# First stages of an attention-and-FFN kernel: transposing loads gated on the first weight chunk, q projections run six tiles behind k, and wq loaded right behind wk

## The chip, the core and the metric

The kernel runs on one core of a Trainium2 chip. The metric is the device time of one execution in microseconds (us). Time before: 278.08 us, the median of 3 runs (277.39 to 278.48).

## The reference, cut to what matters

```python
x = A_x                                            # [1, 2048, 640] bf16
g = sigmoid((x * gate_w).sum(-1, keepdims=True))
qkv = x @ wqkv                                     # wqkv [640, 1920]; 32 heads of 20
pq, pk = phi(q), phi(k)     # phi(t) = where(t > 0, t + 1, exp(t)) + 1e-6
kv = einsum("bhsd,bhse->bhde", pk, v);  z = einsum("bhsd->bhd", pk)
a = (pq @ kv / (pq . z + 1e-6)) @ wo
b = (gelu(x @ w_gate) * (x @ w_up)) @ w_down       # F = 1728
out = g * a + (1 - g) * b
```

The first stage, which the change touches, makes k and q of 16 tiles of 128 rows. For each tile it needs xT, the tile transposed, and the weights wk or wq, which are five chunks (of 128 rows) each.

## The kernel before

Tiles 0 to 2 are loaded plainly and transposed on TensorE (`T`). Tiles 3 to 15 are loaded by transposing DMAs on the SP queue. wk comes on the ACT queue. All k tiles come first, then all q tiles. Item `n` of the sequence uses two PSUM banks out of four pairs, so item n waits for the DVE pass `phi2` of item n-4.

```python
for k in range(KC):                                  # KC = 5
    dma_in(wk[:, k, :], A_wqkv[k*128:(k+1)*128, 640:1280], [r_wk[k]], eng="act")
for i in range(NXN):                                 # NXN = 3, on SP
    dma_in(x_aug[:, i, 0:640], A_x[0, i*128:(i+1)*128, :], [r_xn[i]])
for i in range(NXN, NT):                             # 13 transposing loads, on SP
    load_xT(i)
# ... the other loads, on SP ...
def KM(i, ks):   # k of tile i: per chunk one matmul of 512 and one of 128 columns
    ...          # reads r_xT[i] and r_wk[k]
def QM(i): ...   # q of tile i: reads r_xT[i], r_wq
def phi1(n): ... # ACT: Exp of the two banks
def phi2(n): ... # DVE: two instructions, frees the banks

warm(6, 512)     # six matmuls of 512 columns on a constant
T(0)
warm(2, 128)
T(1)
warm(2, 128)
KM(0, [0])
T(2)
# ... transpose of gate_w ...
KM(1, [0])
for k in range(1, KC):
    KM(0, [k]); KM(1, [k]); KM(2, [k - 1])
KM(2, [KC - 1])
for n in range(2 * NT):
    if n >= NT:  QM(n - NT)
    elif n >= 3: KM(n, list(range(KC)))
    phi1(n)
    phi2(n)
    if n == 3:   # wq, one load of 800 KB, on the ACT queue behind the fourth Exp
        dma_in(wq[:, :, 0:640], A_wqkv[:, 0:640].rearrange(...), [r_wq], eng="act")
```

## Time and profile before

| what | value | view |
|---|---|---|
| PE busy | 270.1 of 275.9 us (98%) | page, busy times |
| chain that ended last | 95% PE | page, chain |
| wk chunk 3: issue to landing | 2.75 to 8.99 us | chain in order of time |
| PE idle at that wait | 0.7 us | waits |
| first k of tile 3, 4, 5 starts | 10.95, 12.32, 13.69 us | timeline, counting pairs |
| k or q of a tile | 5 pairs of 0.27 us = 1.36 us | timeline |

The page: busy time by engine, and the shares of the chain that ended last.

```profile
PE 270.1 (98%) x1663; PEld 140.4 (51%) x1696; DVE 138.5 (50%) x233; ACT 78.3 (28%) x132; POOL 26.1 (9%) x28
...
PE 95%; DMA 2%; issue 1%; ACTq 1%; DVE 0%
```

The chain in order of time (start us, duration us, what): the part before 9 us. The load that it passes through is wk chunk 3.

```profile
2.75 6.24 DMA pool<-in_A_wqkv_dram
...
9.04 0.39 PE ps L419
```

The timeline of PE (start us, duration us, engine, line, operation; in brackets the idle time before and its releaser). L387 is a warm-up, L403 a `T`, L419 the 512-column and L420 the 128-column half of a k pair. In the first pair the halves start 0.42 us apart; from 6.25 us on they start 0.22 us apart, and a pair takes 0.27 us. That is the fastest spacing in these traces, called full rate below.

```profile
4.63 0.42 PE L387 MATMUL ps<-const-bfloat16-1.0 128*128 128x128 bf16 x2
4.85 0.63 PE L419 MATMUL ps<-pool 128*128 128x512 bf16 x1
5.27 0.31 PE L420 MATMUL ps<-pool 128*128 128x128 bf16 x1
5.49 0.71 PE L403 MATMUL ps<-pool 128*128 128x128 bf16 x5
...
6.25 0.39 PE L419 MATMUL ps<-pool 128*128 128x512 bf16 x1
6.47 0.22 PE L420 MATMUL ps<-pool 128*128 128x128 bf16 x1
...
9.04 0.39 PE L419 MATMUL ps<-pool 128*128 128x512 bf16 x1 [0.72 <-DMA pool<-in_A_wqkv_dram]
```

The loads of wk chunk 3 (issued 2.75) and of tile 3's transposing load (issued 2.20), one line each, from the view of DMA issues cut to 2.75 us; the last number is us from issue to landing.

```profile
pool<-in_A_wqkv_dram ACTq DMA_DIRECT2D x1, 160.0 KB, 6.2
pool<-in_A_x_dram SPq DMA_TRANSPOSE x1, 7.3
```

### The profile page before, as it was taken

What the parts mean: (1) busy time and instruction counts of PE and PEld (TensorE: products, weight loads), DVE (VectorE), ACT (ScalarE), POOL (GpSimd) and SP (SyncE); (2) the same over time, 40 slices, a digit from 0 to 9 for tenths busy, and PEclk for the clock granted to TensorE, in tenths of its full rate; (3) what the DMA queues carried; (4) which work ended last, traced back from release to release, by engine and by line L of the source; (5) the groups of instructions that cost most, each with busy time, mean ns of one, the idle gap of its engine ahead of it and who ended that gap; (6) DMA issues with size and microseconds to landing.
All of it is one profiled execution on the core that took longest, in us unless ns stands there. A gap on an engine that the chain in (4) does not pass through costs nothing.

```text
span 275.9 us, 4048 instructions
## 1 busy us (share of the span) xinstructions
PE 270.1 (98%) x1663; PEld 140.4 (51%) x1696; DVE 138.5 (50%) x233; ACT 78.3 (28%) x132; POOL 26.1 (9%) x28
## 2 busy tenths in 40 slices
PE   8899999999999999999999999999999999999996
PEld 5455555555545444444444444444555555555553
DVE  2398888510234324999999998535000122212223
ACT  1355555210431454223222223224555100000000
POOL 5000000000000401242432422000000000000000
PEclk9999999999999999999999999999999999999999
DMA  7998997002120111122121221380000010111111
GB/s 178 172 199 238 395 402 244 12 6 44 23 48 21 50 46 54 25 46 48 26 49 24 47 50 24 60 309 14 0 0 2 24 47 26 48 50 48 50 48 48
DMA packets 36400, 22.38 MB, mean 81 GB/s; under 512 B 25759, under 2 KB 34975, under 8 KB 36383
## 3 DMA queue, kind: packets, MB, share of 16 engines
q1 hardware_dynamic: 34997, 20.49, 27.4%
q10 hardware_dynamic: 1386, 1.64, 2.2%
q8 instruction: 13, 0.21, 0.3%
q14 instruction: 4, 0.03, 0.0%
HBM read 13.11 MB, written 2.62 MB: 57 GB/s over the span
## 4 chain that ended last, share of the span: by engine, by line
PE 95%; DMA 2%; issue 1%; ACTq 1%; DVE 0%
PE ps L596 41%; PE ps L739 20%; PE ps L702 6%; PE ps L432 6%; PE ps L503 6%; PE ps L419 5%; DMA pool<-in_A_wqkv_dram 2%; PE ps L505 2%; PE ps L433 2%; PE ps L703 2%; PE ps L420 2%; PE ps L571 2%; PE ps L723 1%; ACTq L331 1%; PE ps L617 1%
## 5 line engine op out<-in xcount | busy, mean ns | idle before, releaser
L596 PE MATMUL ps<-pool 128*128 128x512 bf16 x509 | 113.0, 379 | 0.6
L596 PEld LDWEIGHTS ps<-pool 128*128 128x128 bf16 x520 | 50.4, 98 | 60.0 <-issue 0.3
L739 PE MATMUL ps<-pool 128*128 128x128 bf16 (+1 forms) x407 | 56.6, 297 | 0.6 <-issue 0.2
L604 DVE TENSOR_TENSOR pool<-ps,pool 128x512 bf16<-128x512 f32 x52 | 35.8, 688 | 33.6 <-PE ps L596 30.4
L602 ACT ACTIVATE pool<-ps 128x512 f32<-128x512 f32 x52 | 31.1, 597 | 72.5 <-PE ps L596 72.1
L750 DVE SCALAR_TENSOR_TENSOR pool<-ps,pool 128x512 bf16<-128x512 f32 (+1 forms) x32 | 16.2, 547 | 63.8 <-PE ps L739 63.8
L739 PEld LDWEIGHTS ps<-pool 128*128 128x128 bf16 x416 | 31.8, 98 | 25.3 <-issue 1.1
L648 POOL TENSOR_TENSOR pool<-pool 128x640 f32<-128x640 bf16 x16 | 22.5, 1409 | 140.1 <-DMA pool<-z_row 87.1
L441 ACT ACTIVATE pool<-ps 128x640 bf16<-128x640 f32 x32 | 22.3, 704 | 23.1 <-PE ps L420 13.5
L454 DVE SCALAR_TENSOR_TENSOR pool<-ps,pool 128x640 bf16<-128x640 f32 x32 | 26.4, 825 | 2.2
L656 DVE TENSOR_TENSOR pool<-pool 128x640 bf16<-128x640 bf16 x16 | 23.0, 1441 | 0.6
L419 PE MATMUL ps<-pool 128*128 128x512 bf16 x77 | 21.9, 383 | 0.7 <-DMA pool<-in_A_wqkv_dram 0.7
L432 PE MATMUL ps<-pool 128*128 128x512 bf16 x77 | 21.4, 379 | 0.0
L702 PE MATMUL ps<-pool 128*128 128x512 bf16 x77 | 21.3, 379 | 0.0
L503 PE MATMUL ps<-pool 128*128 128x512 bf16 x76 | 21.2, 379 | 0.0
L505 PE MATMUL ps<-pool 128*128 128x129 bf16 x80 | 17.6, 220 | 0.2
L420 PE MATMUL ps<-pool 128*128 128x128 bf16 x80 | 17.6, 220 | 0.2
L433 PE MATMUL ps<-pool 128*128 128x129 bf16 x80 | 17.6, 220 | 0.2
L703 PE MATMUL ps<-pool 128*128 128x128 bf16 x80 | 17.5, 219 | 0.2
L707 ACT ACTIVATE pool<-ps,pool 128x640 f32<-128x640 f32 x16 | 12.7, 794 | 9.2 <-PE ps L703 9.2
L451 DVE TENSOR_SCALAR pool<-pool 128x640 bf16<-128x640 bf16 x32 | 10.4, 325 | 7.4 <-ACT pool L441 5.8
L419 PEld LDWEIGHTS ps<-pool 128*128 128x128 bf16 x80 | 7.9, 98 | 10.2 <-DMA pool<-in_A_wqkv_dram 1.0
(51 smaller groups left out, 130.7 us busy)
## 6 DMA issues: line engine op xcount, KB each, us to landing
out_dram<-pool SPq DMA_DIRECT2D x15, 160.0 KB, 1.8
pool<-in_B_w_gate_dram SPq DMA_DIRECT2D x1, 2080.0 KB, 13.6
pool<-in_B_w_up_dram SPq DMA_DIRECT2D x1, 2080.0 KB, 18.3
pool<-in_A_x_dram SPq DMA_DIRECT2D x1, 1280.0 KB, 8.3
pool<-in_B_w_down_dram SPq DMA_DIRECT2D x1, 1120.0 KB, 6.0
pool<-in_A_wo_dram SPq DMA_DIRECT2D x6, 160.0 KB, 8.8
pool<-in_B_w_down_dram SPq DMA_DIRECT2D x1, 960.0 KB, 8.5
pool<-in_A_wqkv_dram ACTq DMA_DIRECT2D x5, 160.0 KB, 4.4
```

Source lines behind the costliest of these rows:

```text
L419: e.matmul(ps[:, b0, :], lhs, wk[:, k, 0:512], start=(k == 0), stop=(k == KC - 1))
L420: last = e.matmul(ps[:, b1, 0:128], lhs, wk[:, k, 512:640], start=(k == 0), stop=(k == KC - 1))
L432: e.matmul(ps[:, b0, :], lhs, wq[:, k, 0:512], start=(k == 0), stop=(k == KC - 1))
L433: last = e.matmul(ps[:, b1, 0:129], lhs, wq[:, k, 512:641], start=(k == 0), stop=(k == KC - 1))
L454: P.op("dve", lambda e: e.scalar_tensor_tensor(dst, ps_flat[:, b0 * 512:b0 * 512 + 640], 1.0 + EPS, e_buf[m], ALU.add, ALU.max), reads=[ba ...
L503: e.matmul(ps[:, bs[n], :], lhs, x_aug[:, i, 0:512], start=(i == 0), stop=(i == NT - 1))
L505: last = e.matmul(ps[:, bt, n * 129:(n + 1) * 129], lhs, x_aug[:, i, 512:641], start=(i == 0 and n == 0), stop=(i == NT - 1), skip_group_c ...
L596: last = e.matmul(ps[:, b, :], w[:, k, fc * 128:(fc + 1) * 128], xT[:, k, j * 512:(j + 1) * 512], start=(k == 0), stop=(k == KC - 1))
L602: P.op("act", lambda e: e.activation(ge[n], ps[:, gb, :], ACT.Gelu_apprx_tanh), reads=[bank[gb]], writes=[r_ge[n]])
L604: P.op("dve", lambda e: e.tensor_tensor(hT[fc][:, j * 512:(j + 1) * 512], ps[:, ub, :], ge[n], ALU.mult), reads=[bank[ub], r_ge[n]], write ...
L702: e.matmul(ps[:, b0, :], lhs, w2[:, m, 0:512], start=(m == 0), stop=(m == KC - 1))
L739: last = e.matmul(dst, lhs, wd[:, fc, c0:c0 + cn], start=False, stop=(fc == NFC - 2), skip_group_check=True)
```

## The change

Its intent: let wk land before the transposing loads start; let q run only six tiles behind k, so that from tile 6 on a new xT is wanted for every second item alone and need not come so fast; and have wq early enough for that.

```diff
+KLEAD = 6
@@ loads
+dma_in(wq[:, :, 0:640], A_wqkv[:, 0:640]..., r_wq, reads=[r_wk[KC - 1]], eng="act")
 for i in range(NXN, NT):
-    load_xT(i)
+    load_xT(i, after=([r_wk[0]] if i == NXN else ()))
@@ order: k0..k5, then q0 k6 q1 k7 ... q9 k15, then q10..q15
+seq = [("k", i) for i in range(KLEAD)]
+for i in range(KLEAD, NT):
+    seq += [("q", i - KLEAD), ("k", i)]
+seq += [("q", i) for i in range(NT - KLEAD, NT)]
@@ head
-warm(6, 512)
+warm(5, 512)
 T(0)
-warm(2, 128)
+warm(3, 128)
 T(1)
-warm(2, 128)
 KM(0, [0])
+KM(1, [0])
 T(2)
 # ... transpose of gate_w ...
-KM(1, [0])
@@ loop
-    if n == 3:
-        dma_in(wq[:, :, 0:640], ..., [r_wq], eng="act")
```

(`phi1`, `phi2` and the bank slots now index `seq`; r_wq became five resources.)

More of the change, by code (lines that the diff above doesn't have):

```diff
@@ L301, in bass_gated_mix__linear_attn_block__geglu_ffn__prompt_kernel @@
             r_wk = [P.sb("wk%d" % k, R_WK + k * 640, R_WK + (k + 1) * 640) for k in range(KC)]
-            r_wq = P.sb("wq", R_WQ, R_WQ + KC * XW)
+            r_wq = [P.sb("wq%d" % k, R_WQ + k * XW, R_WQ + k * XW + 640) for k in range(KC)]
             r_gcol = P.sb("gcol", R_WQ, R_WQ + KC * XW)
@@ L339, in bass_gated_mix__linear_attn_block__geglu_ffn__prompt_kernel @@
                 dma_in(x_aug[:, i, 0:640], A_x[0, i * 128:(i + 1) * 128, :], [r_xn[i]])
+            dma_in(wq[:, :, 0:640], A_wqkv[:, 0:640].rearrange("(k p) w -> p k w", p=128), r_wq,
+                   reads=[r_wk[KC - 1]], eng="act")
             def load_xT(i, after=()):
@@ L410, in T, with KM @@
                     reads=[bank[tb]], writes=[r_xT[i]])
-            def KM(i, ks):
-                b0, b1 = slot(i)
+            seq = [("k", i) for i in range(KLEAD)]
+            for i in range(KLEAD, NT):
+                seq += [("q", i - KLEAD), ("k", i)]
+            seq += [("q", i) for i in range(NT - KLEAD, NT)]
+            def KM(n, ks):
+                i = seq[n][1]
+                b0, b1 = slot(n)
                 def fn(e):
@@ L423, in KM, with QM @@
                 P.op("pe", fn, reads=[r_xT[i]] + [r_wk[k] for k in ks], writes=[bank[b0], bank[b1]])
-            def QM(i):
-                b0, b1 = slot(NT + i)
+            def QM(n):
+                i = seq[n][1]
+                b0, b1 = slot(n)
                 def fn(e):
@@ L435, in fn @@
                     return last
-                P.op("pe", fn, reads=[r_xT[i], r_wq, r_gcol], writes=[bank[b0], bank[b1]])
+                P.op("pe", fn, reads=[r_xT[i], r_gcol] + r_wq, writes=[bank[b0], bank[b1]])
             def phi1(n):
@@ L442, in phi1 @@
                      reads=[bank[b0], bank[b1]], writes=[r_e[m]])
-                if n >= NT:
-                    i = n - NT
+                kind, i = seq[n]
+                if kind == "q":
                     P.op("act", lambda e: e.activation(eg[:, i:i + 1], ps[:, b1, 128:129], ACT.Tanh, scale=0.5),
@@ L452, in phi2 @@
                      reads=[r_e[m]], writes=[r_e[m]])
-                dst, r_dst = (pk[n], r_pk[n]) if n < NT else (pq[n - NT], r_pq[n - NT])
+                kind, i = seq[n]
+                dst, r_dst = (pk[i], r_pk[i]) if kind == "k" else (pq[i], r_pq[i])
                 P.op("dve", lambda e: e.scalar_tensor_tensor(
@@ L476, in bass_gated_mix__linear_attn_block__geglu_ffn__prompt_kernel @@
             for n in range(2 * NT):
-                if n >= NT:
-                    QM(n - NT)
+                if seq[n][0] == "q":
+                    QM(n)
                 elif n >= 3:
@@ L482, in bass_gated_mix__linear_attn_block__geglu_ffn__prompt_kernel @@
                 phi2(n)
-                if n == 3:
-                    dma_in(wq[:, :, 0:640], A_wqkv[:, 0:640].rearrange("(k p) w -> p k w", p=128), [r_wq],
-                           eng="act")
                 if n == 6:
```

## The prediction

> **What bounds the kernel.** TensorE: in the page's busy table PE has 270.1 of 275.9 us, and the chain that ended last is 95% PE. In the waits, PE waits after 12.4 us for nothing but 0.2 us of issue. Only the first 9 us, before the chain is unbroken matmuls, can shrink.
>
> **That start.** The chain runs through the ACT queue's wk loads into wk chunk 3, issued at 2.75 us, landing at 8.99 (6.24 us); its first matmul starts at 9.04, after 0.7 us of PE idle. By the issue-to-landing times the chunks land at about 4.4, 5.7, 6.6, 9.0, 9.4. The first transposing load is issued at 2.20 and lands 7.3 us later. From 2.5 to 5 us there are 85 DMA packets under 512 B and 312 GB/s; from 5 to 6 us, 387 and 207 GB/s, with the DMA share near 1. So transposing packets take the engines when the last wk chunks need them. The Trainium skill, "DMA: Bandwidth & Descriptors", section "Issuing engines are not separate DMA queues", says that loads of all issuers interleave on the same 16 engines; the trace agrees.
>
> **What the change does.**
> 1. Transposing loads start at wk 0's landing, about 4.4 instead of 2.2. Half of wk has moved by 5.0 (queue 10: 0.42 MB); the rest at 300 GB/s takes 1.3 us more: all wk by about 6.5 (estimate).
> 2. PE without waiting for wk: T(0) to T(2) and k of tiles 0 and 1 with chunk 0 until about 6.4; chunk 3's first matmul near 8.2 instead of 9.04. Gain 0.8 to 1.0 us, all critical.
> 3. Two warm-up matmuls fewer (0.43 and 0.21 us): they fill waiting time; about nothing.
> 4. q six tiles behind k: the same matmuls (1.36 us a tile), Exp (0.70), DVE (0.32 + 0.82). xT is wanted half as fast from tile 6 on, but PE did not wait for it before: 0.
> 5. wq is issued at about 6.5 instead of 12.5. Before, it took 7.1 us among transposing loads, so it lands near 14; the first q matmul wants it near 14.0. Stall 0 to 0.6 us, expected 0.2.
> 6. On ACT the wq issue waits for wk 4, ahead of the 1.28 us table load (before: at 3.72, hidden). First Exp not before wk 4 + 0.4 + 1.28, about 8.2; k of tile 0 ends near 9.1: hidden. But tile 4's k already waited for tile 0's DVE pass (0.17 us at 12.31), so beyond about 7.4 each us that wk 4 is later costs PE a us.
> 7. xT3, issued at 4.4 with 3.2 to 5 us to land, is there at 7.6 to 9.4; wanted near 10: small risk.
>
> **Sum.** -0.9 + 0.2 (wq) + 0.1 (xT3, table): about -0.7 us on 278.08, 277.35. Range 276.3 to 278.4 (runs of one kernel spread from 277.39 to 278.48). Within 2%: 0.98; faster 0.01; slower 0.01.
>
> **What would show it.** (1) The last two wk chunks landing in under 5 us; no PE wait for wqkv before 9 us. (2) Every later stage about 0.8 us earlier, with FFN and down-projection lengths unchanged. (4) Unchanged mean durations at the k and q lines. (5) A PE wait for wqkv at 13 to 15 us. (6) A PE wait for DVE before tile 4's k. (7) PE waits for x transposes at tiles 3 to 5.
>
> **What would make it wrong.** wq so slow among the transposes that q of tile 0 waits over 1 us; wk 4 landing near 9, so that the table load shifts Exp and stalls PE; late xT3 to xT5. These could eat the gain; none can reach 2% (5.6 us). A large gain would need PE idle time that the profile does not show.

## The result

| | median us | runs us |
|---|---|---|
| before | 277.80 | 277.34 to 278.48 (6 runs) |
| changed | 278.45 | 277.87 to 279.30 (6 runs) |

The ratio is 1.0023, 95% interval 1.0000 to 1.0046: the same within 2%, but 0.65 us (by the medians) slower where 0.7 us faster was predicted, and just outside the range. A ratio here is the mean time of one kernel's runs over that of the other's of the same rounds, so it is not quite the ratio of the medians. The changed kernel was timed in three more jobs, on three chips (below): 0.9994, 0.9989 and 0.9979. Taken together it is the kernel before within a quarter of a per cent. The question is where the 0.8 to 1.0 us went that should have been gained at the wait for wk.

The traced run of the changed kernel took 279.30 us, the slowest of the six. Its page and, below, its PE timeline (L391 warm-up, L407 `T`, L430 and L431 the k pair):

```profile
PE 273.3 (99%) x1694; PEld 140.6 (51%) x1694; DVE 138.5 (50%) x233; ACT 78.2 (28%) x132; POOL 26.1 (9%) x28
...
PE 97%; DMA 1%; DVE 1%; SPq 0%; issue 0%
```

```profile
3.63 0.53 PE L391 MATMUL ps<-const-bfloat16-1.0 128*128 128x128 bf16 x3
4.95 0.72 PE L407 MATMUL ps<-pool 128*128 128x128 bf16 x5 [0.79 <-DMA pool<-in_A_x_dram]
...
7.55 0.61 PE L430 MATMUL ps<-pool 128*128 128x512 bf16 x1
7.95 0.31 PE L431 MATMUL ps<-pool 128*128 128x128 bf16 x1
8.05 0.63 PE L430 MATMUL ps<-pool 128*128 128x512 bf16 x1
8.48 0.31 PE L431 MATMUL ps<-pool 128*128 128x128 bf16 x1
...
10.19 0.43 PE L430 MATMUL ps<-pool 128*128 128x512 bf16 x1
10.46 0.22 PE L431 MATMUL ps<-pool 128*128 128x128 bf16 x1
10.51 0.38 PE L430 MATMUL ps<-pool 128*128 128x512 bf16 x1
```

The DMA issue of wk chunk 4 in this trace (issued at 3.23 us; the last number is us from issue to landing):

```profile
pool<-in_A_wqkv_dram ACTq DMA_DIRECT2D x1, 160.0 KB, 3.9
```

The wait for wk is gone, as predicted: wk chunk 4 landed in 3.9 us (6.2 before), and no k matmul waits for wqkv. But TensorE is at half rate: until 10.19 us the halves of a pair start 0.40 or 0.43 us apart and a pair takes 0.53 us. After the 0.79 us before `T(1)` PE waits no more, it is just slow; so the page shows it 99% busy. Tile 5's k starts at 15.15 us instead of 13.69, and everything behind it is as long as before: 275.9 - 13.69 = 262.2 and 277.4 - 15.15 = 262.2 us. The view by windows does not tell it from its clock column. Two lines, before (first) and changed (second), for 9 to 10 and 8 to 9 us; the columns are the window, its length, the busy us and (with x) the instructions that ran in it, of PE, PEld, DVE, ACT, POOL, then the granted clock, DMA share and GB/s:

```profile
9.00:10.00 1.00, 0.96 (x7) 0.57 (x8) 0.00 (x0) 0.00 (x0) 0.00 (x0) 1.00 1.28 229
```

```profile
8.00:9.00 1.00, 1.00 (x5) 0.46 (x4) 0.12 (x2) 0.88 (x1) 0.00 (x0) 1.00 1.06 220
```

Both say clock 1.00, yet the second has 5 matmuls in a us where the first has 7 in 0.96 us. The 1.00 is no measurement here: the page of the changed kernel has no PEclk line at all, where that of the kernel before has one, and the column reads 1.00 where a trace holds no record of the clock. The Trainium skill, "TensorE: Matmul & The Clock Gate", Part 1, says that the array runs at half rate until it has been busy for a free-running window of about 3.4 us, and that the same kernel can differ from run to run. The traces here agree as far as they go: the first k pair at full rate is at 10.19 us in this trace of the changed kernel and at 4.85 us in another (a1, below).

### The profile page after: what moved, and what is told of

Its sections match the earlier page's. It is cut to its first block, busy times and chain, and to the rows that moved or that the text cites. A ratio compares the mean times of both kernels' runs of the same rounds, so it can differ in the third digit from the quotient of the medians.

```text
span 277.4 us, 4076 instructions
## 1 busy us (share of the span) xinstructions
PE 273.3 (99%) x1694; PEld 140.6 (51%) x1694; DVE 138.5 (50%) x233; ACT 78.2 (28%) x132; POOL 26.1 (9%) x28
## 4 chain that ended last, share of the span: by engine, by line
PE 97%; DMA 1%; DVE 1%; SPq 0%; issue 0%
PE ps L605 40%; PE ps L748 20%; PE ps L430 7%; PE ps L512 6%; PE ps L444 6%; PE ps L711 6%; PE ps L431 2%; PE ps L445 2%; PE ps L514 2%; PE ps L712 2%; PE ps L580 2%; DMA pool<-in_A_x_dram 1%; PE ps L732 1%; PE ps L626 1%; PE ps L642 1%; PE ps L407 0%
## 5 line engine op out<-in xcount | busy, mean ns | idle before, releaser
L605 PE MATMUL ps<-pool 128*128 128x512 bf16 x520 | 113.7, 379 | 0.0
L748 PE MATMUL ps<-pool 128*128 128x512 bf16 (+1 forms) x416 | 57.2, 299 | 0.0
L453 ACT ACTIVATE pool<-ps 128x640 bf16<-128x640 f32 x32 | 22.3, 703 | 20.7 <-PE ps L431 10.4
L430 PE MATMUL ps<-pool 128*128 128x512 bf16 x80 | 25.0, 401 | 0.1
L444 PE MATMUL ps<-pool 128*128 128x512 bf16 x80 | 23.0, 379 | 0.0
L512 PE MATMUL ps<-pool 128*128 128x512 bf16 x80 | 21.9, 379 | 0.0
L711 PE MATMUL ps<-pool 128*128 128x512 bf16 x80 | 21.8, 379 | 0.0
L431 PE MATMUL ps<-pool 128*128 128x128 bf16 x80 | 18.2, 227 | 0.0
L712 PE MATMUL ps<-pool 128*128 128x128 bf16 x80 | 17.5, 219 | 0.0
L716 ACT ACTIVATE pool<-ps,pool 128x640 f32<-128x640 f32 x16 | 12.7, 793 | 9.2 <-PE ps L712 9.2
L430 PEld LDWEIGHTS ps<-pool 128*128 128x128 bf16 x80 | 8.2, 102 | 10.6 <-issue 1.4
```

Of the source, the lines that this page charges most:

```text
L430: e.matmul(ps[:, b0, :], lhs, wk[:, k, 0:512], start=(k == 0), stop=(k == KC - 1))
L431: last = e.matmul(ps[:, b1, 0:128], lhs, wk[:, k, 512:640], start=(k == 0), stop=(k == KC - 1))
L444: e.matmul(ps[:, b0, :], lhs, wq[:, k, 0:512], start=(k == 0), stop=(k == KC - 1))
L512: e.matmul(ps[:, bs[n], :], lhs, x_aug[:, i, 0:512], start=(i == 0), stop=(i == NT - 1))
L605: last = e.matmul(ps[:, b, :], w[:, k, fc * 128:(fc + 1) * 128], xT[:, k, j * 512:(j + 1) * 512], start=(k == 0), stop=(k == KC - 1))
L711: e.matmul(ps[:, b0, :], lhs, w2[:, m, 0:512], start=(m == 0), stop=(m == KC - 1))
```

## The experiments

All kernels of a group ran on one chip beside the kernel before. All outputs are right. For each traced run I give the start of tile 5's k, counted in pairs on the PE timeline (a pair whose record is missing from the trace, visible as a step of 0.54 us, is counted in). "Slow pairs" are k pairs whose halves start more than 0.3 us apart.

| run | edit | median us (range) | ratio (95%) | slow pairs | tile 5's k starts | span |
|---|---|---|---|---|---|---|
| a1 | changed kernel | 277.76 (277.34 to 278.00) | 0.9994 (0.9981, 1.0008) | 0 | 13.66 | 275.9 |
| a2 | changed, old head | 277.70 (277.46 to 278.00) | 0.9994 (0.9980, 1.0007) | 1 | 13.59 | 275.8 |
| a3 | changed, more warm-ups | 277.86 (277.28 to 278.19) | 0.9996 (0.9982, 1.0011) | 0 | 13.10 | 275.3 |
| a4 | before, new head | 278.06 (277.30 to 278.58) | 1.0000 (0.9982, 1.0018) | 1 | 13.87 | 276.1 |
| b1 | before, gate only | 278.83 (278.54 to 281.69) | 1.0042 (1.0007, 1.0076) | 0 | 13.24 | 276.8 |
| b2 | changed, no gate | 278.54 (278.13 to 278.99) | 1.0016 (0.9996, 1.0036) | 0 | 14.37 | 276.6 |
| b3 | changed, wq moved | 277.88 (276.68 to 279.17) | 0.9999 (0.9966, 1.0031) | 0 | 12.48 | 275.1 |
| b4 | changed, no warm-ups | 278.42 (278.02 to 278.93) | 1.0014 (0.9994, 1.0033) | 6 | 14.39 | 276.6 |
| c1 | wq moved, old head | 277.29 (276.67 to 278.02) | 0.9961 (0.9934, 0.9987) | 0 | 12.45 | 274.7 |
| c2 | wq moved, more warm-ups | 277.14 (276.73 to 277.76) | 0.9955 (0.9931, 0.9980) | 0 | 13.03 | 275.7 |
| c3 | wq moved, wide warm-ups | 277.07 (276.83 to 277.48) | 0.9953 (0.9929, 0.9977) | 0 | 13.26 | 275.5 |
| c4 | changed kernel | 278.18 (277.42 to 279.05) | 0.9989 (0.9960, 1.0018) | 3 | 14.26 | 276.5 |
| d1 | changed kernel | 277.76 (276.99 to 278.24) | 0.9979 (0.9955, 1.0003) | 0 | 13.45 | 275.7 |
| d2 | wq moved | 276.72 (276.56 to 276.98) | 0.9944 (0.9923, 0.9966) | 1 | 12.38 | 274.7 |
| d3 | changed, wide warm-ups | 278.25 (277.29 to 278.89) | 0.9993 (0.9966, 1.0021) | 0 | 14.31 | 276.6 |
| d4 | wq moved, wide warm-ups | 277.64 (276.87 to 278.20) | 0.9974 (0.9950, 0.9999) | 0 | 12.76 | 275.0 |
| e1 | wq moved, no warm-ups | 278.01 (277.28 to 278.94) | 0.9986 (0.9963, 1.0008) | 7 | 14.79 | 277.0 |
| e2 | wq moved | 277.00 (276.77 to 278.76) | 0.9961 (0.9937, 0.9985) | 6 | 14.54 | 276.8 |

One sum holds in every one of these traces within 0.2 us: the span is the start of tile 5's k, plus what PE waits after it in the first stage (0.36 us in b3, 0.47 in c2, both for wq; 1.37 in b1; under 0.1 elsewhere), plus 262.2 us. So only what sets tile 5's start, and these late waits, matter.

### Group a: is it the slow start of TensorE?

The theory after the first trace: the new head leaves PE idle before `T(1)`, so full rate comes late. The rivals: x tile 1 merely landed late in that run; or the gate, the early wq or the new order costs the time.

```diff
# a1: the changed kernel, unedited
# a2: the changed kernel with the head of before
# a3: the changed kernel with
-warm(3, 128)
+warm(9, 128)
 T(1)
+warm(4, 128)
 KM(0, [0])
# a4: the kernel before with the head of the changed kernel
```

> The changed kernel again, for a second trace. Clock theory (the new head leaves TensorE idle around the wait for x tile 1, so the switch to full matmul rate, seen in the trace as pairs of 0.27 us in place of 0.53, comes near 10 us instead of 5.5): the trace again shows several k pairs at 0.53 us after 6.5 us, and the time is 0.3 to 1 us above before. Delivery theory (x tile 1 simply landed late, 4.9 us, in the one trace we have): x tile 1 lands near 4.0 here, k pairs are fast from 6 us on, and this trace's span is at or under before's 275.9.

> The changed kernel with the old head (six 512-column warm-ups, then two and two of 128 columns; tile 1's first k after T(2)). Clock theory: full rate at about 5.5 us again, and the gain that was predicted shows: 0.5 to 1 us under before, about 277.0. Rival (the DMA gate, the early wq load or the interleaved q cost the time): still 0.3 to 1 us over before, as the changed kernel.

> The changed kernel with nine 128-column warm-ups after T(0) in place of three and four after T(1). Clock theory: no idle before 6 us, full rate at about 5.5 us, 0.5 to 1 us under before although about 1 us of matmuls was added. Delivery theory or DMA rival: no gain over the changed kernel, or worse by up to the added 0.6 to 1.1 us.

> The kernel before with only the new head. Clock theory: full rate comes later than 5.5 us here too; but k pairs before 9.0 us only eat time that was spent waiting for wk chunk 3, so 0 to 1.5 us over before. Rival: equal to before within 0.3 us.

The theory fell as the explanation of the usual run. In a1 full rate came before the first k pair (4.85 us), no pair was slow, and the gain was still missing: 0.9994. The old head (a2) and more warm-ups (a3) gave 0.9994 and 0.9996, not the 0.5 to 1 us that the theory expected; a4 was equal to before.

The trace of a1 shows where the gain went. Tile 4's k starts at 11.30 us, 1.02 us earlier than before: the predicted gain is there. Tile 4's first matmul, before (first) and in a1 (second), from the PE timelines:

```profile
12.32 0.39 PE L419 MATMUL ps<-pool 128*128 128x512 bf16 x1
```

```profile
11.30 0.39 PE L430 MATMUL ps<-pool 128*128 128x512 bf16 x1
```

Then tile 5's k waits. PE timeline of a1 (L430, L431 as above):

```profile
12.40 0.38 PE L430 MATMUL ps<-pool 128*128 128x512 bf16 x1
12.62 0.22 PE L431 MATMUL ps<-pool 128*128 128x128 bf16 x1
13.66 0.38 PE L430 MATMUL ps<-pool 128*128 128x512 bf16 x1 [0.82 <-DVE pool L463]
```

The bracket names DVE, but the DVE pass that frees these two banks, item 1's, had ended at 12.33 us. Where the engine named had long been done, look for a DMA: the DMA issues of a1, cut to 7.4 us, show wq (issued 7.15) and tile 5's transposing load (issued 7.35):

```profile
pool<-in_A_wqkv_dram ACTq DMA_DIRECT2D x1, 800.0 KB, 6.0
pool<-in_A_x_dram SPq DMA_TRANSPOSE x1, 6.2
```

wq lands at 13.14, tile 5's xT at 13.52 (the expectation of b3 below says 13.65), its matmul starts at 13.66. The transposing load of tile 4, issued at 6.04, 1.1 us before wq, had landed in 3.1 us. So a second theory: a transposing load that is issued about when a large plain load goes out, or while it is in flight, lands only about when that plain load lands. It fits the kernel before too (tile 3's xT at 9.5, after wk's last chunks). In the first trace of the changed kernel the same happened: wq landed at 12.28 us, the xT of tile 4 (issued 0.7 us before wq) at 12.43 and that of tile 5 at 12.82, but PE was so late (15.15) that nobody waited.

The view of DMA queues shows that the engines did not simply share. For 8.7 to 10.9 us of a1 it has one line, the ACT queue's, which carried wq (packets, MB, share of the 16 engines), and none for the SP queue:

```profile
q10 hardware_dynamic: 501, 0.64, 90.4%
```

So no packet of the transposing loads of tiles 5 and 6, issued at 7.35 and 8.67, started in these 2.2 us. In a2, where tile 5's load was issued 0.5 us before wq, the SP queue moved 0.49 MB, as much as the loads of tiles 3 to 5, from 5.57 to 9.5 us, and tile 5's load still landed only at 13.5 us, after wq (13.1). Why is not known.

### Group b: the collision of wq with the transposing loads

```diff
# b3: wq on the SP queue, right behind the third transposing load
-dma_in(wq[:, :, 0:640], ..., r_wq, reads=[r_wk[KC - 1]], eng="act")
 for i in range(NXN, NT):
     load_xT(i, after=([r_wk[0]] if i == NXN else ()))
+    if i == 5:
+        dma_in(wq[:, :, 0:640], ..., r_wq)
# b1: the kernel before, with the gate alone
-    load_xT(i)
+    load_xT(i, after=([r_wk[0]] if i == NXN else ()))
# b2: the changed kernel without the gate (the inverse of b1's edit)
# b4: the changed kernel without warm(5, 512) and warm(3, 128)
```

> The changed kernel with the wq load issued on the SP queue right behind the transposing loads of tiles 3 to 5, in place of the ACT queue behind wk. Collision theory (a transposing load that is issued while wq is in flight lands only when wq has landed; in the second trace of the changed kernel tile 5's load, issued at 7.4, landed at 13.65, and its k matmul started at 13.66): tile 5's load lands near 10.5, its first k matmul starts at 12.6 to 12.9, the loads of tiles 6 and on land just after wq at about 14.5, q of tile 0 waits 0 to 0.5 us, and the kernel is 0.5 to 1.0 us under before. Rival (clock start alone decides, or the DMA engines are simply full until 13.6): tile 5's load still lands after 13 us and the time stays within 0.3 us of before.

b3's trace did what the collision theory says: tile 5's load, issued at 7.37, landed in 2.9 us, its k started at 12.48 us without a wait, q of tile 0 waited 0.36 us for wq, and the load of tile 6, now behind wq, landed at about the time of wq (14.7 and 14.1 us). The times did not follow so simply. They fell in two groups: 276.68, 276.98, 277.16 and 278.61, 278.66, 279.17, so the mean is before's. The traced run was one of the first group. ("Slow run" below means the second group.)

> The kernel before with the transposing loads gated on wk chunk 0, and nothing else. Collision theory: wk lands by 7.5 us and tile 4's k starts about 1 us earlier, but wq, still issued near 12 us, holds back the transposing loads behind it, about tile 9, until it lands near 18 us; TensorE waits 0.5 to 2 us there, so the kernel is 0 to 1 us over before. Rival (the gate itself is the gain, as predicted): 0.7 to 1.0 us under before, no wait for x transposes.

The gate alone makes the kernel slower, by 0.42% in the mean (one run of 281.69 us is in it) and 0.3% by the medians. Tile 5's k starts at 13.24 us, 0.45 earlier than before (about 1 us was expected); then tile 8's k waits for its xT. The PE timeline of b1 (L419, L420 the k pair):

```profile
17.04 0.38 PE L419 MATMUL ps<-pool 128*128 128x512 bf16 x1
17.26 0.22 PE L420 MATMUL ps<-pool 128*128 128x128 bf16 x1
18.68 0.38 PE L419 MATMUL ps<-pool 128*128 128x512 bf16 x1 [1.20 <-DVE pool L451]
```

and the DMA issues of b1 at 12.2 us, wq (issued 12.07, landed about 18.8) and the transposing load of tile 8 (issued 11.47, landed about 18.5):

```profile
pool<-in_A_wqkv_dram ACTq DMA_DIRECT2D x1, 800.0 KB, 6.7
pool<-in_A_x_dram SPq DMA_TRANSPOSE x1, 7.1
```

They land together within 0.2 us. This is the collision at another place, where wq stands in the kernel before. The expectation named tile 9; it was tile 8, because a load issued 0.6 us before wq is caught as well (in b2 even one issued 0.8 us before; in the kernel before, one issued 0.9 us before wq landed in 4.0 us). The kernel before escapes it: there the transposing loads started 2.6 us earlier, so that the ones caught by wq belong to later tiles, and PE was 0.45 us later. Gate and early wq thus belong together; but where the early wq was put it only moved the wait from tile 8 to tile 5.

> The changed kernel without the gate. wk chunks 3 and 4 land near 9.0 and 9.5 us as before; the wq issue on ACT waits for chunk 4, and the table load and the first Exp come behind it at about 11.2 instead of 10.3, so tile 4's k waits for DVE 0.6 to 0.9 us: 0.5 to 1 us over before. If the order on ACT does not matter: within 0.3 us of before.

Without the gate the kernel is 0.5 us over before by the medians, with an interval that includes 1. In its trace the order of the ACT queue costs time: wk chunk 4 lands near 9.3 us again, wq and then the table load wait for it, and tile 4's k waits 0.8 us for DVE. The ACT timeline of b2 (L332 a load, L453 the table load and Exp):

```profile
1.38 8.31 ACTq L332 DMA_DIRECT2D pool<-in_A_wqkv_dram  x6
9.72 1.28 ACT L453 ACT_TABLE_LOAD   x1 [9.72 <-DMA pool<-in_A_wqkv_dram]
11.02 2.49 ACT L453 ACTIVATE pool<-ps 128x640 bf16<-128x640 f32 x4
```

In a1, with the gate, the table load ends at 8.84 us and the first Exp starts at 9.33 us, when PE has k of tile 0 ready: hidden, as predicted.

> The changed kernel without any warm-up matmul, to measure a late clock start by itself. Clock theory: k pairs take 0.53 us until 8 to 10 us, tile 5's k starts at 14.5 to 15.5 us in place of 13.7, the time is 0.7 to 1.8 us over the changed kernel's. Rival (warm-ups do nothing for the rate): pairs at 0.27 us from the first on and a time equal to the changed kernel's, about before's.

Without warm-ups six pairs are slow, full rate comes at 9.15 us, and tile 5's k starts at 14.39. Tile 5's xT had landed at about 13.3, so here PE's own pace set the start. The cost over a1's 13.66 (another chip, one trace each) is 0.7 us, the low end of what was expected, since the wait for tile 5 had been there anyway. In these two traces a slow start and the late xT do not add; the later of the two counts.

### Groups c and d: both repairs, and the two by two

```diff
# c1: b3 with the head of before;   c2: b3 with a3's warm-ups
# c3 and d4: b3 with wide warm-ups;   d3: the changed kernel with them
-warm(3, 128)
+warm(3, 512)
 T(1)
+warm(2, 512)
 KM(0, [0])
# c4 and d1: the changed kernel;   d2: b3 again
```

> wq behind tile 5's transposing load, and the old head. Its predecessor with the new head had runs of 276.7 to 277.2 and runs of 278.6 to 279.2. Clock theory (the new head's idle before T(1) makes the full rate come late in some runs): with the old head no run over 278, median 276.8 to 277.3, 0.6 to 1.1 us under before. Rival (the two groups of runs come from the loads, not from the head): runs still fall into two groups 2 us apart.

> wq behind tile 5's transposing load, and nine 128-column warm-ups after T(0), four after T(1). Clock theory: as the old head or better, one group of runs, median 276.6 to 277.2, no k pair over 0.3 us after 6.5 us. Rival: two groups of runs 2 us apart.

> wq behind tile 5's transposing load, and warm-ups of 512 columns between the transposes (three after T(0), two after T(1)), about 1 to 2 us of added matmuls at the slow rate. Clock theory: one group of runs; the added matmuls delay T(1) by up to 0.7 us, which costs 0 to 0.7 us against the version with 128-column warm-ups: median 276.8 to 277.6. Rival: two groups of runs 2 us apart.

> The changed kernel a third time, for the spread of its runs and a third trace. If late full rate and the wait for tile 5's transposing load are its two costs: each trace shows tile 5's k starting at 13 to 13.8 us with early full rate, or near 15 with late full rate; the span is that start plus 262.2 us within 0.2; runs lie between 277.2 and 279.3. If something else costs the time, the span does not follow that sum.

With wq moved, all three heads are faster than before, by 0.39 to 0.47%, with intervals that exclude 1, and none shows two groups of runs. c1's slowest run (278.02) is just over the 278 that was expected as a limit. c4's tile 5 starts at 14.26 us, between the 13 to 13.8 and the 15 that were expected. Its trace names the wait without an error. The PE timeline of c4, the last pair of tile 4 and the first of tile 5:

```profile
12.99 0.22 PE L431 MATMUL ps<-pool 128*128 128x128 bf16 x1
14.26 0.38 PE L430 MATMUL ps<-pool 128*128 128x512 bf16 x1 [1.05 <-DMA pool<-in_A_x_dram]
```

wq was issued at 7.40 and landed in 6.3 us (13.7); tile 5's load was issued at 7.03 and landed in 7.1 us (14.12).

> The changed kernel. Two-cause theory: median 277.7 to 278.5, runs up to 279.3; tile 5's k starts at 13.6 us or later.

> wq moved, new head. Two-cause theory: runs between 276.7 and 279.2, more than 1.5 us of spread, the fast ones about 1 us under the changed kernel's fast ones. If the head is not the cause of the slow group: spread as small as with wide warm-ups, on this chip.

> The changed kernel with wide warm-ups (three of 512 columns after T(0), two after T(1)). Two-cause theory: the slow runs go, but tile 5's k still starts at 13.1 to 14.2 us, held by its transposing load: median 277.3 to 278.0, no run over 278.5.

> Both repairs. Two-cause theory: median 276.9 to 277.3, no run over 277.8, tile 5's k at 12.9 to 13.3 us with no wait for x transposes; 0.3 to 0.8 us under the wide warm-ups alone, and under before in the same rounds. If moving wq was worth nothing: equal to the wide warm-ups alone.

On one chip, moving wq is worth 1.04 us with the new head (277.76 to 276.72) and 0.61 us with wide warm-ups (278.25 to 277.64), by the medians. The edit changes wq's queue and place together; it also takes wq off the ACT queue, ahead of the table load. In the traces, tile 4's k starts at 11.20 us in d1 and at 11.01 in d2, and tile 5's k waits 0.88 us in d1 and not in d2: most of the gain is the collision. A wq load that stays on the ACT queue and is only issued later was not tried. The DMA issues of d2 at 7.3 us show tile 5's load alone, issued at 7.07:

```profile
pool<-in_A_x_dram SPq DMA_TRANSPOSE x1, 3.0
```

and the PE timeline of d2 shows tile 5's first pair, at 12.38, following tile 4's last without a wait (L429, L430 the k pair):

```profile
12.11 0.38 PE L429 MATMUL ps<-pool 128*128 128x512 bf16 x1
12.32 0.22 PE L430 MATMUL ps<-pool 128*128 128x128 bf16 x1
12.38 0.38 PE L429 MATMUL ps<-pool 128*128 128x512 bf16 x1
```

The other half of the expectation failed: d2, with the new head, had no slow group here (276.56 to 276.98), and the wide warm-ups cost 0.5 to 0.9 us instead of saving something. d3's runs reached 278.89 although none over 278.5 was expected, and d4, at 277.64 with runs up to 278.20, missed its 276.9 to 277.3; in d3's trace no pair was slow, but wq took 6.8 us and tile 5's k waited until 14.31.

### Group e: what the slow group is

```diff
# e1: b3 without warm(5, 512) and warm(3, 128);   e2: b3 again
```

> wq behind tile 5's load, new head, no warm-ups at all. If late full rate is what the slow group was: k pairs at 0.53 us until about 9 us, tile 5's k near 14.2 us with no wait for x transposes, median 278.0 to 279.0, so 1.3 to 2.2 us over the same kernel with warm-ups. If the slow group was something else: within 0.5 us of that kernel.

> wq behind tile 5's load, new head, a third time. Collision theory: fast runs at 276.5 to 277.2, 0.5 to 1.2 us under before; if late full rate strikes, some runs near those without warm-ups.

By chance e2's traced run was its only slow one: 278.76, the other five being 276.77 to 277.27. The PE timeline of that run:

```profile
8.30 0.63 PE L429 MATMUL ps<-pool 128*128 128x512 bf16 x1
8.73 0.31 PE L430 MATMUL ps<-pool 128*128 128x128 bf16 x1
8.84 0.63 PE L429 MATMUL ps<-pool 128*128 128x512 bf16 x1
9.26 0.26 PE L430 MATMUL ps<-pool 128*128 128x128 bf16 x1
9.36 0.38 PE L429 MATMUL ps<-pool 128*128 128x512 bf16 x1
9.57 0.22 PE L430 MATMUL ps<-pool 128*128 128x128 bf16 x1
```

Six slow pairs, full rate at 9.36 us, tile 5's k at 14.54, no wait for x transposes or wq. The fast runs of the same kernel that were traced (b3, d2) have full rate by the second pair and start tile 5 at 12.4 to 12.5 us. So this slow run is a run with late full rate; the slow runs of b3 were not traced. It costs 2.1 us at tile 5, and 1.8 us of the time (278.76 against 276.99, the mean of the other five). Without warm-ups (e1) the median is 278.01, 1.0 us over e2's, less than the 1.3 to 2.2 that was expected: e1's runs lie between 277.28 and 278.94, so it seems that full rate does not come equally late in each.

Which head makes late full rate likely stays open. With the new head, 3 of the 9 traces have three or more slow pairs (the first one, c4, e2); with the old head or more warm-ups, none of 9. That suggests the head, but d2 had six fast runs with it. The two worst traces had PE idle for 0.79 and 0.52 us before `T(1)`, because x tile 1 landed late; a1 and b3 idled 0.36 and 0.31 us there and were fast. But b2 idled 0.64 us there and had no slow pair, and c4 did not idle there and had three: the idle time alone does not tell.

## Why the prediction was wrong

- **What bounds the kernel, and how much was to be had: right.** Only the start can shrink; the rest is 262.2 us in all traces. PE's wait for wk was the place, and removing it brought tile 4's k forward by 1.02 us (a1; 0.52 in a2 to 1.12 in d1), where 0.8 to 1.0 was predicted.
- **Step 1, wk lands early: right in kind, a little off in size.** The last two chunks took 3.9 to 4.0 us instead of 6.2; all wk by 7.1 to 7.2 us (a1 and the first trace), where 6.5 was estimated.
- **Steps 5 and 7 are the ones that failed.** Step 5 asked how much the transposing loads would delay wq ("Stall 0 to 0.6 us, expected 0.2"); wq came in time, at 13.14 us in a1. The delay went the other way. Step 7 took "3.2 to 5 us to land" for the transposing loads from loads that had no wq in flight, reckoned with tile 3 alone ("small risk"), and gave it, with the table, 0.1 us. The prediction did name "late xT3 to xT5" among what could make it wrong, but not wq as their cause. Tile 3's load indeed took 3.8 us in a1, but tile 5's took 6.2 us, because it was issued 0.2 us after wq, and its k started at 13.66 instead of 12.66 (tile 4's start plus 1.36). That term, put at 0.1 us, is 1.0 us in a1 (0.4 us in a2 and a3, 0.9 in d1, 1.2 in c4 and d3). It is the gain, given back. Moving wq behind that load won 1.04 us (d1 against d2; 0.61 us with wide warm-ups). The 7.3 us that tile 3's load took in the profile of before, beside wk, could have warned: it looks like the same collision.
- **Step 3, two warm-up matmuls fewer "about nothing": wrong in some runs.** It counted warm-ups as filler, and did not ask what they do for the rate. In the traced run full rate came at 10.19 us and tile 5's k at 15.15, 1.5 us later than in a1. That is the slowest of the first six runs. The spans of the other five are 276.0 to 276.8 us, so by the sum above their tile 5 started at 13.8 to 14.6 us, about 14.3 at the median. They were not traced. In c4 and d3 the wait for tile 5's xT reached such a start (14.26 and 14.31) with full rate in time, so which of the two causes put the median of the first job at 278.45 stays open. In the three later jobs the medians were 277.76, 278.18 and 277.76, inside the range, but with no gain on before of the same rounds beyond 0.2%.
- **Step 6, the table load behind wq: right.** It was hidden with wk landing at 7.1 us, and cost 0.8 us of PE where wk landed near 9.3 (b2).
- **Step 4, the new order worth 0 by itself: not tested alone.** b1 shows what it is for: with the gate and the old order, tile 8's xT is late.
- **Within 2%, probability 0.98: right.**

The version that is faster than before in six of seven jobs is the changed kernel with wq on the SP queue behind tile 5's load. With the new head it was 0.9999, 0.9944 and 0.9961 of before in three jobs; with one of the other heads 0.9953 to 0.9974 in four. It is 0.6% at best, not the 2% that would count as clearly faster.

## What to carry to other kernels

When a change moves a load forward, list every load that will then be in flight beside it, and take each one's time from a stretch of the trace where it had such company; here tile 5's transposing load took about 3 us with no large plain load in flight and 5 to 7 us beside one. Order loads by when their first reader wants them, across queues: tile 5's xT, wanted at 12.7 us, stood behind wq, wanted at 14. And at the start of a kernel, look at the spacing of matmuls, not only at busy time or the clock column: half-rate matmuls fill the busy time and show no wait.

## What the Trainium skill lacked or had wrong

- "DMA: Bandwidth & Descriptors", section "Queues, rings and completion order", says that each DMA engine takes turns between queues packet by packet. From that one would expect a transposing load and a plain one to share. Here tile 5's transposing load landed 0.4 us after the 800 KB wq load that went out within 0.4 us of it on another queue (a1: 13.14 and 13.52 us; c4: 13.74 and 14.12), and in a1 no packet of its queue started for 2.2 us while wq's queue moved 0.64 MB; a load issued 1.3 us before wq was not held (d2: landed in 3.0 us). The mechanism was not found, and the section has nothing on a plain load that keeps the packets of a transposing one from starting. What it says of completion signals, that they wait for earlier writes of the same DMA engine on every queue, might bear on the late landing in a2; that was not tested.
- "Advanced Engine Details and Errata", section "X-Bar Transpose (TRN2)", says that transposing DMAs are as fast as regular ones. Here transposing loads alone moved 270 GB/s (the kernel before, 9.5 to 10.5 us, DMA share 1.28), and the plain wq load alone moved 369 GB/s in the same microsecond of a1 (share 1.01): about a quarter less. And tile 5's transposing load took 5.1 to 7.1 us beside wq, against 2.9 to 3.4 us with wq behind it.
- "TensorE: Matmul & The Clock Gate", Part 1, holds that the ramp is under 1% of a typical kernel and not to be fitted to a count of slow matmuls. That is so here too (1.8 us of 277 in e2, 0.6%), but it is more than the whole change was worth, and it sets one run of e2 apart from the other five. Part 1 also warns not to trust a trace's clock events fully; here they are missing: the changed kernel's page has no PEclk line, and its clock column reads 1.00 at half rate, from 8 to 9 us.
